# The stores of the output, issued by ScalarE at one place of the unit instead of by SyncE between the loads

## The chip, the cores and the metric

The kernel runs on one core of a Trainium2 chip. The metric is the device time of the whole kernel in microseconds. A verdict of faster or slower needs more than 2%.

## The reference

Attention over 8 batches, 12 heads, 448 positions and 64 columns a head, with one added to the softmax's denominator, and behind it one two-layer network with the activation h * tanh(softplus(h)) (Mish) on 3584 rows.

```python
scores = scale * np.matmul(q, k.transpose(0, 1, 3, 2))
m = np.max(scores, axis=-1, keepdims=True)
e = np.exp(scores - m)
attn = e / (np.sum(e, axis=-1, keepdims=True) + np.exp(-m) + 1e-09)
x = np.matmul(attn, v)           # heads side by side: [3584, 768]
h = x @ w_in                     # [768, 2048]
g = h * np.tanh(softplus(h))
out = g @ w_out                  # [2048, 768], float32
```

## The kernel before

The work is cut into units. A unit is three pairs of heads, half of a batch, so that there are 16 units of attention, u = 0 to 15 in the code. A batch's network can start when both of its units are done, so the first product with Mish runs two units behind the attention, and the second product later still. From u = 2 on a unit's stretch holds attention for itself, the end of the attention of the unit before, and the network for earlier batches. Units 16 to 19 hold the network alone.

All engines issue in the order in which the code is written. From u = 6 (`JOINED_FROM`, the seventh unit) that order is one list of steps, `JOINED`, and the loop at L738 walks it. Its steps: `s` writes scores to PSUM banks on TensorE, `m` takes row maxima on VectorE (L335), `e` the exponentials on ScalarE (L347; A and B are the two heads, the number is the step within the unit, of 12), `fill` runs two of sixteen matmuls of the second product (L543), `copy` moves finished parts of it from PSUM to an output buffer `o_sb` on VectorE (L522), `av` and `avc` are the weights times V and their copy to `xT` (L423, L432). `load` issues three loads of a pair of heads, q, k and v, on SyncE (L158), and for the second and third pair has GpSimd cast an earlier one (L201 to L207, L188). `turn` has SyncE issue a transposing DMA of one pair's q and k (L237).

Behind the list come the exponential of the maxima (L360), then the stretch from L841: eight products of the first layer (L442), each with its Mish on ScalarE (L469, L481), and between them the denominators (L363) and the normalising on VectorE and GpSimd (L386, L384), three transposing DMAs of the normalised weights on SyncE (`eT`, L390) and the transposes of the next q and k on TensorE (L224). The PSUM banks are assigned by hand: the fourth of the products goes into the bank that step 9's first head used.

A block of 128 output rows is done when 24 parts of its width have been copied. `evac` (L517) then calls `store_rows` (L495), which issues two DMAs for the block (a block spans two segments of the output), of 48 to 336 KB. They go out on SyncE's queue, at the `copy` step: behind `load` 1 and ahead of `load` 2 for the parts of `copy` 1, behind `load` 2 for those of `copy` 2. In the units u = 6, 10 and 14 one block is finished, in the other seven of u = 6 to 15 two: 17 blocks, 34 DMAs. The very last block, in pieces, has one of each two DMAs on ScalarE's queue already (L502).

`ld_pool` has four buffers for each of q, k and v, `o_pool` four.

Of the kernel before, what the change touches and what calls it, by code (L numbers as in the profile page):

```python
# [19 lines left out]
def kernel(  # L20
# [9 lines left out]
    nc = tc.nc  # L30

    B, H, S, D = q.shape
    d_model, d_ff = moe_w_in.shape
# [102 lines left out]
    def flush_late():  # L136
        while late:
            late.popleft()()
        late.extend(later)
        later.clear()  # L140

    def mo_take():

        while not mo_free:
            flush_late()
        return mo_free.popleft()
# [87 lines left out]
    def turn_by_dma(p):  # L234

        qk = qk_all[:, p % UNIT_PAIRS]
        nc.sync.dma_start_transpose(  # L237
            out=qk.rearrange("c s (t q) -> c (s t) q", q=SP_),
            in_=qk_bf[:, p % N_CAST].rearrange("q s t h d -> q (s t h d)"),
        )  # L240
        qkT[p] = qk[:, 0, :], qk[:, 1, :]
# [87 lines left out]
    def score_maxima(st, s, at, heads=(0, 1)):  # L329
        sc, cols = st["sc", s]  # L330
        maxima = [(st["negm"][:, c : c + 1], sc[bk][:, 0:S]) for bk, c in enumerate(cols) if bk in heads]
        if len(cols) == 2 and sc_pairs[at] is not None:
            maxima = [(st["negm"][:, s : s + 5 : 4], sc_pairs[at][:, :, 0:S])]
        for negm, scored in maxima:
            nc.vector.tensor_reduce(out=negm, in_=scored, axis=AX.X, op=ALU.max, negate=True)  # L335

    def exps(idx, heads=(0, 1)):
        p, s = divmod(idx, STEPS)
        if p >= N_PAIRS:
            return  # L340
        st = att[p]
        sc, cols = st["sc", s]
        rg["used"] -= 1
        for bk, c in enumerate(cols):
            if bk not in heads:
                continue
            nc.scalar.activation(  # L347
                out=st["en"][:, :, c, 0:SP_],
                in_=sc[bk][:, 0:S].rearrange("q (j c) -> q j c", j=NT),
                func=AF.Exp, bias=st["negm"][:, c : c + 1], scale=1.0,  # L350
                accum_out=st["sums"][:, c : c + 1],
            )
        if s == STEPS - 1 and p < HP:
            nc.scalar.activation(out=st["expm"], in_=st["negm"], func=AF.Exp)
        elif s == STEPS - 1 and p % UNIT_PAIRS == UNIT_PAIRS - 1 and p // UNIT_PAIRS < JOINED_FROM:
            expm_of(p)
# [56 lines left out]
    def av_pair(p, act=False, bank=None):  # L413
        b, hp = p // HP, p % HP
        eT = att[p]["eT"]
        v_bf = casted[p][2]
        if b not in xT:
            xT[b] = xT_pool.tile([128, DM_T, S], BF16, tag="xT", name="xT")
        av = mo_take() if bank is None else bank
        for j in range(NT):  # L420
            for h in range(2):
                e_h = eT[0:SP_, j, h * S : (h + 1) * S]
                nc.tensor.matmul(  # L423
                    av[h * 64 : (h + 1) * 64, 0:S],
                    lhsT=v_bf[:, h, j * D : (j + 1) * D],
                    rhs=e_h,
                    start=(j == 0), stop=(j == NT - 1),
                )
        copy = nc.scalar.copy if act else nc.vector.tensor_copy

        def evac():
            copy(out=xT[b][:, hp, :], in_=av[:, 0:S])  # L432
            if bank is None:
                mo_free.append(av)

        del att[p], casted[p], qkT[p]
        return evac
# [54 lines left out]
            out=mids[g][:, :, 64 * half : 64 * half + 64], in_=gT[b][:, :, at : at + 64]  # L492
        )

    def store_rows(g, i, o_sb, cols):  # L495

        parts, r = [], i * 128
        while r < (i + 1) * 128:
            n = min((i + 1) * 128, (r // SP_ + 1) * SP_) - r
            parts.append((r, n))  # L500
            r += n
        queues = [nc.sync, nc.scalar if (g, i) == (B // 2 - 1, 6) else nc.sync]  # L502
        for queue, (r, n) in zip(queues, sorted(parts, key=lambda part: -part[1])):
            seg = r // SP_
            b, t, c0 = 2 * g + seg // NT, seg % NT, r % SP_
            rows = out[b * S : (b + 1) * S, :].rearrange("(c t) m -> t c m", t=NT)
            queue.dma_start(
                out=rows[t, c0 : c0 + n, cols], in_=o_sb[r - i * 128 : r - i * 128 + n, cols]
            )
# [3 lines left out]
    def mm2_group(pieces, bank=None):  # L513

        st = {"at": 0, "o": bank, "evacs": []}

        def evac(g, i, q0, nq, at, last):  # L517
            cols, n_cols = slice(q0 * NQ, (q0 + nq) * NQ), nq * NQ
            if (g, i) not in o_sbs:
                o_sbs[g, i] = [o_pool.tile([128, d_model], FP32, tag="o_sb", name="o_sb"), 0]  # L520
            o_sb, have = o_sbs[g, i]
            nc.vector.tensor_copy(out=o_sb[:, cols], in_=st["o"][:, at : at + n_cols])  # L522
            if last and bank is None:
                mo_free.append(st["o"])
            o_sbs[g, i][1] = have + nq
            if (g, i) == (B // 2 - 1, 6):
                store_rows(g, i, o_sb, cols)
            elif have + nq == 24:
                store_rows(g, i, o_sb, slice(0, d_model))

        def chunk(k, f0, f1):
            g, i, q0, nq = pieces[k]
            if st["o"] is None:
                flush_late()
                st["o"] = mo_take()
            if i < 3:
                src, c0 = gT[2 * g], i * 128
            elif i == 3:
                src, c0 = mids[g], 0
            else:  # L540
                src, c0 = gT[2 * g + 1], i * 128 - S
            for ff in range(f0, f1):
                nc.tensor.matmul(  # L543
                    st["o"][:, st["at"] : st["at"] + nq * NQ],
                    lhsT=src[:, ff, c0 : c0 + 128],
                    rhs=w_out_sb[:, ff, q0 * NQ : (q0 + nq) * NQ],
                    start=(ff == 0), stop=(ff == FF_T - 1),
                )
            if f1 == FF_T:
                last = k == len(pieces) - 1  # L550
                args = (g, i, q0, nq, st["at"], last)
                st["evacs"].append(lambda: evac(*args))
                st["at"] += nq * NQ
                if last and bank is None:
                    late.extend(st["evacs"])

        step = 2
        chunks = [
            (lambda k=k, f0=f0: chunk(k, f0, f0 + step), pieces[k][3] / 6)
            for k in range(len(pieces))  # L560
            for f0 in range(0, FF_T, step)
        ]
        return chunks, st["evacs"]
# [8 lines left out]
    for g in range(B // 2):  # L572
# [61 lines left out]
        ("eB", 6), ("load", 2), ("fill", 1), ("m", 11), ("fill", 1), ("eB", 5), ("fill", 1),  # L634
# [4 lines left out]
    )  # L639
    PART_BANK = (7, 6, 2)  # L640
    AV_BANK = (7, 3, 6)
# [79 lines left out]
    for u in range(UNITS_PER_B, N_UNITS + 2 * UNITS_PER_B):  # L721
# [16 lines left out]
        for what, arg in JOINED if joined else ():  # L738
            at, idx = p0 + arg, p0 * STEPS + arg
            heads = {"A": (0,), "B": (1,)}.get(what[-1], (0, 1))  # L740
            if what == "s":
                held[arg] = score_products(idx)
            elif what[0] == "m":
                score_maxima(*held[arg], heads)
            elif what[0] == "e":
                exps(idx, heads)
            elif what == "fill":
                for _ in range(arg):
                    filler.popleft()[0]()
            elif what == "copy":  # L750
                for evac in copies[arg]:
                    evac()
            elif what == "av":
                held["av", arg] = av_pair(at - UNIT_PAIRS, bank=joined_banks[AV_BANK[arg]])
            elif what == "avc":
                held["av", arg]()
            elif what == "load":
                load_pair(at + LEAD - 1)
                if arg:
                    cast_pair(at + LEAD - 2)  # L760
            elif nxt + arg in TURN_BY_DMA:
                turn_by_dma(nxt + arg)
# [3 lines left out]
        for n in () if joined else range(steps):  # L766
            pi, s = divmod(n, STEPS)
# [73 lines left out]
        for f in range(FF_U):  # L841
# [4 lines left out]
            if moe:  # L846
                first = to_group and nxt == GROUP_FROM
                bank, ff = sc_banks[0][0] if f == 1 else None, w * FF_U + f
                if joined:
                    bank = joined_banks[JOINED_MISH_BANK[f]]  # L850
                elif to_group:
                    at = (FIRST_MISH_BANK if first else MISH_BANK)[f]
                    if at is not None:
                        bank = (sc_banks[0][1], None, mo_tiles[1], sc_banks[0][0])[at]
# [71 lines left out]
```

## Time and profile before

| | |
|---|---|
| runs | 464.16, 464.88, 459.46 us (median 464.16) |
| the profiled execution | 462.32 us; its span 460.5 us, mean granted clock 0.989 |
| TensorE busy | 427.1 us, 93% |
| VectorE, ScalarE busy | 340.7 and 342.3 us, 74% each |
| GpSimd busy | 185.7 us, 40% |
| DMA packets | 92.66 MB, mean 201 GB/s |
| units u = 6 to 15, start of the second product's first group | 145.92, 170.33, 198.50, 222.90, 247.65, 273.28, 297.68, 322.43, 346.90, 372.41 us |

Lines such as L347 are lines of the kernel. In the rows of a timeline the first number is the start and the second the duration in us; what stands in brackets is the idle time of the engine just before and what ended it. SPq and ACTq are the sequencers that issue DMAs; a DMA's row there is its issue alone, not the movement of its data. The span runs from the first to the last instruction; the execution's own time is 1.8 us longer.

### The profile page before, as it was taken

Reading aid. Unit: us, or ns where it says so; the run is one execution under the profiler, and the core shown is the slowest. Engines: PE = TensorE matmul, PEld = TensorE weight load, DVE = VectorE, ACT = ScalarE, POOL = GpSimd, SP = SyncE. Lnnn points to the kernel's source line nnn. Section 1 sums busy time; section 2 is a strip of 40 time slices with the busy share of each in tenths; the row PEclk is TensorE's granted clock in tenths of the full one; section 3 lists DMA queues with packets and bytes.
Section 4 is the critical chain, followed back from the end, with each engine's and each line's share of the span. In section 5 each row is a group of like instructions: output and inputs, shape, how many; then the busy total and the mean of one; then the engine's idle time right before and its main releaser. Section 6 shows DMA issues by size and latency. Waiting matters only on the chain.

```text
span 460.5 us, 8732 instructions
## 1 busy us (share of the span) xinstructions
PE 427.1 (93%) x2968; PEld 234.4 (51%) x2968; DVE 340.7 (74%) x756; ACT 342.3 (74%) x908; POOL 185.7 (40%) x352
## 2 busy tenths in 40 slices
PE   4586798899999999899999999999999999999996
PEld 2243445444445555455555545564555455555565
DVE  4899968878797888668788888888888888421021
ACT  5998988988797788688888887897979878211300
POOL 3666839253517161534436271715454360000000
PEclk9997999999999999999999999999999999999999
DMA  8999999997999989998999999999999995950213
GB/s 210 220 202 221 282 188 248 200 212 174 223 263 217 246 171 227 266 207 234 185 270 211 219 227 206 247 219 254 229 265 201 244 206 135 177 133 0 70 36 103
DMA packets 211661, 92.66 MB, mean 201 GB/s; under 512 B 168352, under 2 KB 208160, under 8 KB 211616
## 3 DMA queue, kind: packets, MB, share of 16 engines
q1 hardware_dynamic: 204032, 85.76, 87.4%
q0 software_dynamic: 7488, 6.29, 9.3%
q8 instruction: 23, 0.38, 0.3%
q14 instruction: 22, 0.18, 0.1%
q10 hardware_dynamic: 96, 0.05, 0.0%
HBM read 45.61 MB, written 11.01 MB: 123 GB/s over the span
## 4 chain that ended last, share of the span: by engine, by line
PE 65%; DMA 10%; DVE 9%; ACT 6%; issue 3%; SPq 3%; POOL 2%; POOLq 0%; DVEq 0%
PE mo L543 24%; PE mo L442 17%; DMA q_f<-in_q_dram 7%; PE b L442 7%; DVE negm L335 6%; PE b L543 5%; ACT en L347 5%; PE b L304 4%; PE mo L423 2%; DMA k_f<-in_k_dram 2%; PE b L224 2%; PE b L423 2%; DMA eT<-en 1%; PE mo L312 1%; DVE xT L432 1%
## 5 line engine op out<-in xcount | busy, mean ns | idle before, releaser
L347 ACT ACTIVATE en<-b,negm 128x448 bf16<-128x448 f32 x216 | 133.9, 636 | 20.9 <-DVE negm L335 20.9
L335 DVE TENSOR_REDUCE negm<-b 128x1 f32<-128x448 f32 x216 | 120.6, 614 | 21.2 <-PE b L307 21.2
L543 PE MATMUL mo<-w_out_sb,gT 128*128 128x384 bf16 (+3 forms) x736 | 107.5, 298 | 2.4 <-DVE o_sb L522 1.8
L543 PEld LDWEIGHTS <-gT 128*128 128x128 bf16 x896 | 82.4, 98 | 51.8 <-issue 10.5
L442 PEld LDWEIGHTS <-w_in_sb 128*128 128x128 bf16 x768 | 72.6, 98 | 67.7 <-issue 7.3
L442 PE MATMUL mo<-xT,w_in_sb 128*128 128x448 bf16 x480 | 102.7, 357 | 0.8 <-DVE xT L432 0.3
L481 ACT ACTIVATE gT<-mo 128x448 bf16<-128x448 f32 x73 | 40.2, 551 | 54.1 <-PE mo L442 53.7
L384 POOL TENSOR_SCALAR en<-en,rden 128x448 bf16<-128x448 bf16 x109 | 67.3, 634 | 23.5 <-DVE rden L378 15.5
L386 DVE TENSOR_SCALAR en<-en,rden 128x448 bf16<-128x448 bf16 x227 | 71.5, 384 | 0.7
L442 PE MATMUL b<-xT,w_in_sb 128*128 128x448 bf16 x282 | 58.8, 353 | 0.2 <-DVE xT L432 0.2
L347 ACT ACTIVATE en<-sc,negm 128x448 bf16<-128x448 f32 x84 | 52.5, 642 | 4.0 <-DVE negm L335 2.6
L522 DVE COPY o_sb<-mo 128x384 f32<-128x384 f32 (+3 forms) x54 | 25.8, 492 | 40.0 <-PE mo L543 39.4
L335 DVE TENSOR_REDUCE negm<-sc 128x2 f32<-128x896 f32 (+1 forms) x48 | 45.2, 966 | 6.0 <-PE sc L307 4.0
L203 POOL TENSOR_SCALAR qk_bf<-q_f 112x512 bf16<-112x512 f32 x18 | 11.1, 615 | 90.5 <-DMA q_f<-in_q_dram 90.5
L347 ACT ACTIVATION_READ_ACCUMULATOR en<-b,negm 128x1 f32 x216 | 45.1, 209 | 0.0
L188 POOL CAST v_bf<-v_f 112x512 bf16<-112x512 f32 x48 | 29.7, 619 | 14.1 <-DMA v_f<-in_v_dram 13.3
L201 POOL CAST qk_bf<-q_f 112x512 bf16<-112x512 f32 x29 | 19.2, 662 | 37.2 <-DMA q_f<-in_q_dram 36.9
L207 POOL CAST qk_bf<-k_f 112x512 bf16<-112x512 f32 x47 | 29.1, 618 | 6.0 <-DMA k_f<-in_k_dram 5.4
L224 PEld LDWEIGHTS <-qk_bf 112*128 112x128 bf16 x304 | 19.8, 104 | 22.2 <-DVE qk_bf L201 4.4
L423 PEld LDWEIGHTS <-v_bf 112*64 112x64 bf16 x384 | 20.1, 110 | 19.5 <-issue 9.2
L543 PE MATMUL b<-w_out_sb,gT 128*128 128x384 bf16 x160 | 29.3, 326 | 0.0
L304 PE MATMUL b<-qk_all 64*128 64x448 bf16 x108 | 29.0, 355 | 0.0
(71 smaller groups left out, 523.7 us busy)
## 6 DMA issues: line engine op xcount, KB each, us to landing
q_f<-in_q_dram SPq DMA_DIRECT2D x48, 224.0 KB, 5.3
k_f<-in_k_dram SPq DMA_DIRECT2D x48, 224.0 KB, 5.4
v_f<-in_v_dram SPq DMA_DIRECT2D x48, 224.0 KB, 5.6
w_in_sb<-in_moe_w_in_dram POOLq DMA_DIRECT2D x12, 256.0 KB, 6.1
w_out_sb<-in_moe_w_out_dram POOLq DMA_DIRECT2D x8, 384.0 KB, 7.7
out_dram<-o_sb SPq DMA_DIRECT2D x7, 336.0 KB, 5.1
out_dram<-o_sb SPq DMA_DIRECT2D x8, 288.0 KB, 4.8
out_dram<-o_sb SPq DMA_DIRECT2D x8, 240.0 KB, 5.4
```

The source lines that it names most:

```text
L188: nc.gpsimd.tensor_copy(out=casted[p][2], in_=loaded.pop(p)[2])
L207: cast_k(out=k_bf, in_=k_f.rearrange(by_t, t=NT))
L224: nc.tensor.transpose(by_s[s][:, t * SP_ : (t + 1) * SP_], src[:, t].rearrange("p h d -> p (h d)"), ident[:SP_, :SP_],)
L304: nc.tensor.matmul(sc[0][:, 0:S], lhsT=qT[0:64, qa : qa + 128], rhs=kA, start=True, stop=True)
L335: nc.vector.tensor_reduce(out=negm, in_=scored, axis=AX.X, op=ALU.max, negate=True)
L347: nc.scalar.activation(out=st["en"][:, :, c, 0:SP_], in_=sc[bk][:, 0:S].rearrange("q (j c) -> q j c", j=NT), func=AF.Exp, bias=st["negm"][ ...
L384: nc.gpsimd.tensor_scalar(scalar2=1.0, op0=ALU.mult, op1=ALU.mult, **args)
L386: nc.vector.tensor_scalar(scalar2=None, op0=ALU.mult, **args)
L423: nc.tensor.matmul(av[h * 64 : (h + 1) * 64, 0:S], lhsT=v_bf[:, h, j * D : (j + 1) * D], rhs=e_h, start=(j == 0), stop=(j == NT - 1),)
L442: nc.tensor.matmul(h_ps[:, 0:S], lhsT=w_in_sb[:, dm, ff * 128 : (ff + 1) * 128], rhs=xT[b][:, dm, :], start=(dm == 0), stop=(dm == DM_T - 1),)
L481: nc.scalar.activation(out=gT[b][:, ff, :], in_=h_ps[:, 0:S], func=AF.Mish)
L543: nc.tensor.matmul(st["o"][:, st["at"] : st["at"] + nq * NQ], lhsT=src[:, ff, c0 : c0 + 128], rhs=w_out_sb[:, ff, q0 * NQ : (q0 + nq) * NQ ...
```

## The change

Blocks that are finished in units from u = 6 to 15 are no longer stored at the `copy` step. They are noted in a list, and a new step `store`, at one place late in `JOINED`, issues all of them on ScalarE's queue. In ScalarE's order the place is behind the exponentials `eA 8` and ahead of `eB 9`; three more exponentials follow. In SyncE's order nothing is left of these 34 DMAs. The stores of u = 5 and before, and of u = 16 to 19, stay where they are.

```diff
+    to_store = []
+
-    def store_rows(g, i, o_sb, cols):
+    def store_rows(g, i, o_sb, cols, queue=nc.sync):
...
-        queues = [nc.sync, nc.scalar if (g, i) == (B // 2 - 1, 6) else nc.sync]
+        queues = [queue, nc.scalar if (g, i) == (B // 2 - 1, 6) else queue]
...
             elif have + nq == 24:
-                store_rows(g, i, o_sb, slice(0, d_model))
+                if bank is None:
+                    store_rows(g, i, o_sb, slice(0, d_model))
+                else:
+                    to_store.append((g, i, o_sb, slice(0, d_model), nc.scalar))
...
-        ("mB", 8), ("s", 9), ("mB", 9), ("avc", 2), ("eB", 9), ("mA", 9), ("eB", 8), ("mB", 10),
-        ("eA", 9), ("eB", 10), ("turn", 1),
+        ("mB", 8), ("s", 9), ("mB", 9), ("avc", 2), ("store", 0), ("eB", 9), ("mA", 9),
+        ("eB", 8), ("mB", 10), ("eA", 9), ("eB", 10), ("turn", 1),
...
+            elif what == "store":
+                while to_store:
+                    store_rows(*to_store.pop(0))
```

## The prediction

> I count units as the code does, from u = 0, so the seventh is u6. The ones that change are u6 to u15. In each of them the loads come as three pairs of heads; I call their transfers q0 k0 v0, q1 k1 v1, q2 k2 v2, the stores S1, S2 (one finished block of 128 rows) or S1 to S4 (two), and "the hold" the time that ScalarE is kept from its next exponential by the stores.
>
> **What bounds the kernel now.** First the page: TensorE is busy for 93% of the span and carries most of the chain that ended last; DMA carries a tenth of it.
>
> ```profile
> span 460.5 us, 8732 instructions
> PE 427.1 (93%) x2968; PEld 234.4 (51%) x2968; DVE 340.7 (74%) x756; ACT 342.3 (74%) x908; POOL 185.7 (40%) x352
> PE 65%; DMA 10%; DVE 9%; ACT 6%; issue 3%; SPq 3%; POOL 2%; POOLq 0%; DVEq 0%
> ```
>
> Then the stretches from the first matmuls of one unit's second product (the group of 32) to the next unit's: u6, u7, u10, u11 and u14. The columns are length, then busy time of PE, PEld, DVE, ACT and POOL, then the granted clock.
>
> ```profile
> 145.92:170.33 24.41, 24.41 (x174) 13.54 (x175) 21.07 (x49) 20.91 (x57) 10.06 (x21) 1.00 1.03 203
> 170.33:198.50 28.17, 26.38 (x174) 13.86 (x175) 20.62 (x48) 21.09 (x57) 14.01 (x27) 0.94 1.09 237
> ...
> 247.65:273.28 25.63, 24.75 (x174) 13.57 (x175) 21.79 (x49) 21.21 (x57) 11.58 (x24) 1.00 1.05 220
> 273.28:297.68 24.40, 24.40 (x174) 13.54 (x175) 20.84 (x48) 20.91 (x57) 10.91 (x22) 1.00 1.10 233
> ...
> 346.90:372.41 25.51, 24.34 (x166) 13.08 (x167) 21.96 (x48) 20.58 (x56) 10.91 (x22) 1.00 1.18 222
> ```
>
> A unit that nothing disturbs takes 24.40 us, all of it TensorE. So the nine units u6 to u14 (145.92 to 372.41, 226.5 us) hold only 226.5 - 9 x 24.40 = 6.9 us that any change of order could win, over half of it in u7. But two loops run close beside TensorE. The first is SyncE's queue, here in u11 with its start in the unit before:
>
> ```profile
> 268.03 13.82 SPq L390 DMA_TRANSPOSE eT<-en  x3
> 281.91 0.57 SPq L158 DMA_DIRECT2D q_f<-in_q_dram  x1
> ...
> 283.02 0.46 SPq L158 DMA_DIRECT2D v_f<-in_v_dram  x1
> 283.52 0.46 SPq L158 DMA_DIRECT2D q_f<-in_q_dram  x1
> 284.02 0.46 SPq L158 DMA_DIRECT2D k_f<-in_k_dram  x1
> 284.52 0.46 SPq L158 DMA_DIRECT2D v_f<-in_v_dram  x1
> 285.08 2.31 SPq L507 DMA_DIRECT2D out_dram<-o_sb  x4
> 287.84 0.49 SPq L158 DMA_DIRECT2D q_f<-in_q_dram  x1
> 288.85 0.34 SPq L158 DMA_DIRECT2D k_f<-in_k_dram  x1
> 289.64 0.31 SPq L158 DMA_DIRECT2D v_f<-in_v_dram  x1
> 290.30 1.27 SPq L237 DMA_TRANSPOSE qk_all<-qk_bf  x1
> 293.23 4.35 SPq L390 DMA_TRANSPOSE eT<-en  x1
> ```
>
> The transposes of the attention weights fill the queue for 13.8 us, and the loads can't start before. The second thing to see is the gaps ahead of q2, k2 and v2 (287.39 to 287.84, 288.33 to 288.85, 289.19 to 289.64). The waits of SyncE's queue in this unit name what ended them:
>
> ```profile
> SPq L158 <- DMA q_f<-in_q_dram: 0.5, 1, 0.5
> SPq L158 <- DMA k_f<-in_k_dram: 0.4, 1, 0.4
> SPq L158 <- DMA v_f<-in_v_dram: 0.4, 1, 0.4
> ```
>
> A load needs none of those transfers. GpSimd's casts, which do need them, tell when they landed:
>
> ```profile
> 287.94 0.61 POOL L188 CAST v_bf<-v_f 112x512 bf16<-112x512 f32 x1 [0.88 <-DMA v_f<-in_v_dram]
> 288.88 0.61 POOL L201 CAST qk_bf<-q_f 112x512 bf16<-112x512 f32 x1 [0.33 <-DMA q_f<-in_q_dram]
> 289.68 0.61 POOL L207 CAST qk_bf<-k_f 112x512 bf16<-112x512 f32 x1 [0.18 <-DMA k_f<-in_k_dram]
> 290.35 0.61 POOL L188 CAST v_bf<-v_f 112x512 bf16<-112x512 f32 x1
> ```
>
> q2 left when v0 had landed, k2 when q1 had, v2 when k1 had. Count the issues: v0 q1 k1 v1 S1 S2 S3 S4 q2. **Each issue waits until the transfer eight issues before it has landed.** This rule decides the case.
>
> **The change, part by part.** It takes 17 blocks, 34 DMAs, from SyncE, where they stood ahead of q2 or behind v2, and puts them on ScalarE's queue behind eA 8 and ahead of eB 9. What an issue costs:
>
> ```profile
> L507 SPq DMA_DIRECT2D out_dram<-o_sb x57: 316/424/1673, 129.9 to 457.4; - x57
> L507 ACTq EVENT_SEMAPHORE  x3: 17/17/17, 436.2 to 456.5; - x3
> L507 ACTq DMA_DIRECT2D out_dram<-o_sb x3: 376/377/395, 453.7 to 457.4; - x3
> ```
>
> Removed: about 0.42 us of SyncE's queue per store, so q2 leaves some 2.8 us sooner in u11 (behind v1 at 285.0) and lands sooner too, since the stores' data no longer go first. That ends most of the excess of u7, u10 and u14. Added on ScalarE: 0.38 us of issue per store. ScalarE has a place for it:
>
> ```profile
> 260.52 0.20 ACT L347 ACTIVATION_READ_ACCUMULATOR en<-b,negm 128x1 f32 x1
> 262.17 0.63 ACT L347 ACTIVATE en<-b,negm 128x448 bf16<-128x448 f32 x1 [1.45 <-DVE negm L335]
> ...
> 286.15 0.20 ACT L347 ACTIVATION_READ_ACCUMULATOR en<-b,negm 128x1 f32 x1
> 287.80 0.63 ACT L347 ACTIVATE en<-b,negm 128x448 bf16<-128x448 f32 x1 [1.45 <-DVE negm L335]
> ```
>
> In u10 and u11 alike it idles 1.45 us ahead of eB 9. Two issues (0.76) hide there and four (1.5) all but hide; without that cover they would be 12.9 us for all 34.
>
> **The wait that moves with them** is the cost. The question is whether ScalarE's issues count in the same eight. The trace's own records of the last issues of the kernel name the semaphore that each DMA signals on:
>
> ```
> 451.07 SP 109   451.61 SP 101   453.67 ACT 102   453.67 SP 103   454.79 SP 104
> 455.16 SP 105   456.11 ACT 107   456.10 SP 108   457.43 ACT 109   457.43 SP 101
> ```
>
> One rotation of eight (106 is no DMA's) serves both queues, and each of the three ACT issues has a wait instruction of its own ahead of it (the x3 row). So I take it that a store on ScalarE waits for the eighth DMA before it, whoever issued that one. The order around the place is eT eT eT, nine loads, the qk transpose, the stores. Eight back from S1 is v0, from S2 q1, from S3 k1, from S4 v1. ScalarE then stands still until q1 (two stores) or v1 (four) has landed, though the blocks that it stores were copied long before. In u11 that is 290.35 + 0.38 = 290.73 against 287.80 now: a hold of 2.9 us.
>
> Behind the waiting store on ScalarE are eB 9, eB 8, eA 9, eB 10, the exponential of the maxima, the table load and the first Mish. TensorE waits for eA 9's bank: the fourth product of the next stretch goes there, and its start is 288.10 + 2 x 1.14 = 290.4 by the row below, 0.7 us after eA 9 ends now (287.80 + 1.9). All but 0.7 us of the hold is TensorE's.
>
> ```profile
> 288.10 3.57 PE L442 MATMUL b<-xT,w_in_sb 128*128 128x448 bf16 x18
> ```
>
> Worse, it closes a loop: the loads land, ScalarE goes on, the sums and the normalising follow, the transposes are issued, then the next loads. From eB 9 to the first transpose takes 268.03 - 262.17 = 5.86 us; from there to v1 in hand 290.35 - 268.03 = 22.3, to q1 20.9. With the last issue (0.38) a turn of the loop is 28.6 us for four stores and 27.1 for two. In u9 it is shorter:
>
> ```profile
> 218.34 4.89 SPq L390 DMA_TRANSPOSE eT<-en  x1
> 239.84 0.61 POOL L188 CAST v_bf<-v_f 112x512 bf16<-112x512 f32 x1
> ```
>
> 21.5 to v1, so 27.7 with the same rest. I take the middle, 28.1 and 26.5. All this exceeds 24.40, so the loop, not TensorE, sets the pace. The turns that end in u7, u8, u9, u11, u12 and u13 have four stores, those in u10 and u14 two; u15 has no loads and goes free. Six at 28.1 and two at 26.5 make 221.6 us, where 346.90 - 145.92 = 201.0 stand now (the gains on q2 are swallowed in this). That is +20.6; the first hold, in u6, adds under 1, and the last slack of 0.7 is given back.
>
> Unknown costs. (a) S1 starts while q1 to v1 are under way and may slow them: from nothing to the 384 KB of a block at the 233 GB/s of u11's row, 1.6 us a turn; I take nothing, since the other side is as open: (b) if the qk transpose is counted behind S4, the wait ends with k1, 0.7 us sooner a turn. (c) An issue may meet an issue of SyncE: none to 1.27 us, the qk transpose's row; I take none, as that one starts about when v1 lands. Of this the Trainium skill speaks (Perfetto Trace Analysis, "DMA Instruction — HWDGE (DVE, Sync)"): the descriptor generator is shared by the issuing sequencers and locked for one at a time. By it the stores would cost up to a SyncE issue each, which would put the sum towards the high end; no row of this case shows such a lock.
>
> The sum against the profiled execution's own 462.3 us: 462.3 + 20.6 = **483 us**. The median of the runs shown is 464.2, so this reads as 4% slower.
>
> **Rivals.** *No hold* (not slower): ScalarE's issues do not wait for loads, because their count is kept apart. For it: 1.45 us of cover at just that place. Against it: the common rotation. Then the 6.9 us is open, less what TensorE waits in u10 for k1, which stands ahead of the stores in any case,
>
> ```profile
> 267.04 0.37 PE L224 MATMUL b<-ident,qk_bf 112*128 112x112 bf16 x4 [0.80 <-POOL qk_bf L207]
> ```
>
> and some 0.6 elsewhere: 462.3 - 5.5 = 457 us. It holds where the wait of S4 ends less than 0.7 us after eB 9's present start. The Trainium skill gives this outcome (DMA: Bandwidth & Descriptors, "Issuing engines are not separate DMA queues"): issuing from several engines saves only the sequencer's time to initiate, usually small. The 0.42 us row agrees with "small"; the rule leaves the wait ahead of an issue out.
>
> *Short hold*: in the counted order the third pair and the qk transpose come behind the stores, so S4 waits for v0 and S2 for q0. The turn with four stores is then 287.94 - 268.03 + 0.38 + 5.86 = 26.2 us, with two TensorE's 24.40: 6 x 26.2 + 2 x 24.4 - 201.0 = +5, or 467 us. Against it: without stores in front SyncE reaches q2 before ScalarE reaches the place (285.0 against 286.35).
>
> *Hold and cold clock*: now TensorE waits once for more than 1 us, in u7, and is granted about half its clock behind that.
>
> ```profile
> 192.99 0.37 PE L224 MATMUL b<-ident,qk_bf 112*128 112x112 bf16 x4 [1.61 <-POOL qk_bf L201]
> ...
> 194.00:196.00 2.00, 2.00 (x8) 0.85 (x7) 0.00 (x0) 0.98 (x2) 1.75 (x7) 0.62 1.28 290
> ```
>
> u7's 26.38 us busy against 24.41 in u6 put that at 2.0 us a unit. With such a wait in every unit the late products can delay GpSimd's share of the normalising, and with it the third transpose and the loop. If half of it enters each turn, it is 483 + 8 x 1.0 = 491 us. For the forecast I leave it out, since a turn of 28.1 has 3.7 us to spare over 24.40.
>
> **How the numbers follow.** Forecast 0.72, no hold 0.13, short hold 0.07, cold clock 0.08. The forecast's own range, from (b) on all eight turns and u9's shorter turn (475) to half of (a) (490), is 475 to 490. To hold 8 in 10 I take 466 to 495: it takes in the short hold and the cold clock and leaves out no hold. Two per cent, about what a measurement of this kernel tells from no change, is 454.9 to 473.4 about the median. Forecast and cold clock, less a little, give slower 0.77; no hold and short hold give same 0.20; 0.03 is left for faster.
>
> **What would show it.** Right: ScalarE's idle ahead of eB 9 grows from 1.45 to 3 us and more, units of 27 to 29 us from u7 to u14 and 24 in u15, TensorE waiting at L442 on ScalarE's exponentials, SyncE's queue idle ahead of the first transpose. Wrong: eB 9 still 14.5 us behind the start of its unit, and units of 24.40. Then the rotation does not bind ScalarE, and the waits for q2 will be gone from the chain.

## The result, and the profile after

The changed kernel takes 482.74 us (median of 4 runs, 480.21 to 488.37) beside 461.81 us (4 runs, 458.14 to 464.88) for the kernel before: a ratio of 1.044, interval 1.031 to 1.056. It is slower by 20 us. The ratio leaves out the run of 488.37 us, over 1.5% above the fastest; the profile shown is that of a second set of runs of the same kernel, from an execution of 482.67 us. Two of the lines have moved with the edit: the stores' L507 is now L509, the second product's L543 is L548.

First the page: span, busy times and the chain that ended last.

```profile
span 480.5 us, 8708 instructions
PE 430.8 (90%) x2968; PEld 236.1 (49%) x2968; DVE 332.5 (69%) x756; ACT 342.3 (71%) x908; POOL 185.0 (39%) x352
PE 49%; DMA 15%; SPq 13%; ACT 9%; DVE 7%; issue 3%; ACTq 1%; POOL 1%; POOLq 0%; DVEq 0%
```

The span is 20.0 us longer and hardly any of that is work: ScalarE's 342.3 us are the same to the digit, TensorE has 3.7 us more. In the chain TensorE has gone from 65% to 49%, and the transfers with SyncE's queue from 13% to 28%. This is what a path looks like that no longer runs through the busiest engine. TensorE's waits say where it joins that path:

```profile
PE b L442 <- ACT en L347: 20.3, 9, 4.2
PE sc L304 <- ACT en L347: 9.9, 13, 1.5
```

The second row stood there before with 10.0 us; the first is new, with nine waits, one in each of u6 to u14. In these nine units TensorE now waits for 20.5 us, all but 0.2 of it in the new row, where it waited for 4.1 (for GpSimd, L224). These 16.4 us and 3.1 us more of busy time (225.40 against 222.29) are the 19.5 us that the nine units have grown by. Next the timeline of ScalarE in u11, in which one row holds the case:

```profile
294.82 0.20 ACT L347 ACTIVATION_READ_ACCUMULATOR en<-b,negm 128x1 f32 x1
297.72 3.19 ACTq L509 DMA_DIRECT2D out_dram<-o_sb  x4
300.96 0.63 ACT L347 ACTIVATE en<-b,negm 128x448 bf16<-128x448 f32 x1 [5.95 <-DMA v_f<-in_v_dram]
```

eB 9 comes 5.95 us after the accumulator's read ends, 1.45 before. The four issues stand in 3.19 us, though four of the same row's median (0.36) would be 1.4: there is time between them. GpSimd's casts of the same unit say what that time is:

```profile
297.82 0.61 POOL L188 CAST v_bf<-v_f 112x512 bf16<-112x512 f32 x1 [1.03 <-DMA v_f<-in_v_dram]
298.66 0.61 POOL L201 CAST qk_bf<-q_f 112x512 bf16<-112x512 f32 x1 [0.22 <-DMA q_f<-in_q_dram]
299.56 0.61 POOL L207 CAST qk_bf<-k_f 112x512 bf16<-112x512 f32 x1 [0.29 <-DMA k_f<-in_k_dram]
300.53 0.61 POOL L188 CAST v_bf<-v_f 112x512 bf16<-112x512 f32 x1 [0.35 <-DMA v_f<-in_v_dram]
```

These are v0, q1, k1 and v1, each 0.05 to 0.12 us after it landed. By the trace's records of the semaphores they landed at 297.70, 298.61, 299.51 and 300.41 us, and the single issues are S1 297.72, S2 298.63, S3 299.53 and S4 300.43. So ScalarE issues one store for each load that lands. It is like this throughout: all 30 stores of u6 to u14 leave 0.02 us (one 0.09) after the landing of the DMA that last used their semaphore. SyncE's queue closes the loop:

```profile
270.87 1.36 SPq L237 DMA_TRANSPOSE qk_all<-qk_bf  x1
278.34 4.17 SPq L390 DMA_TRANSPOSE eT<-en  x1
...
294.89 0.46 SPq L158 DMA_DIRECT2D v_f<-in_v_dram  x1
295.39 0.46 SPq L158 DMA_DIRECT2D q_f<-in_q_dram  x1
...
306.10 4.83 SPq L390 DMA_TRANSPOSE eT<-en  x1
```

It is idle for 6.1 us ahead of the first transpose (272.23 to 278.34), and q2 now leaves right behind v1, at 295.39. From one first transpose to the next are 27.8 us. Last the stretches u6, u7, u10, u11 and u15, with the columns as before:

```profile
146.43:171.13 24.70, 24.55 (x176) 13.51 (x174) 20.49 (x49) 20.86 (x57) 10.21 (x21) 1.00 1.06 205
171.13:201.41 30.28, 26.22 (x176) 14.28 (x174) 19.78 (x48) 21.15 (x57) 13.66 (x27) 0.94 1.05 207
257.16:281.87 24.71, 24.55 (x175) 13.53 (x174) 20.59 (x49) 20.89 (x57) 8.92 (x19) 1.00 1.01 206
281.87:311.63 29.76, 25.98 (x175) 14.15 (x174) 19.79 (x48) 21.14 (x57) 13.55 (x27) 0.94 1.08 204
392.41:416.04 23.63, 23.00 (x153) 12.64 (x152) 20.56 (x51) 20.06 (x54) 3.11 (x7) 1.00 0.76 158
```

### The profile page after: what moved, and what is told of

It reads as the page before. It is cut to its first block, busy times and chain, and to the rows that moved or that the text cites. A ratio compares the mean times of both kernels' runs of the same rounds, so it can differ in the third digit from the quotient of the medians.

```text
span 486.2 us, 8708 instructions
## 1 busy us (share of the span) xinstructions
PE 431.8 (89%) x2968; PEld 236.9 (49%) x2968; DVE 333.4 (69%) x756; ACT 341.8 (70%) x908; POOL 185.5 (38%) x352
## 4 chain that ended last, share of the span: by engine, by line
PE 48%; DMA 20%; SPq 14%; ACT 10%; DVE 3%; issue 2%; POOL 1%; ACTq 1%; POOLq 0%; DVEq 0%
PE mo L548 17%; PE mo L442 15%; SPq L390 9%; DMA v_f<-in_v_dram 8%; ACT en L347 8%; PE b L442 7%; DMA eT<-en 5%; DMA k_f<-in_k_dram 5%; SPq L158 5%; PE b L304 2%; PE b L224 2%; DMA q_f<-in_q_dram 2%; DVE negm L335 2%; PE b L423 1%; ACTq L509 1%
## 5 line engine op out<-in xcount | busy, mean ns | idle before, releaser
L347 ACT ACTIVATE en<-b,negm 128x448 bf16<-128x448 f32 x216 | 133.9, 638 | 50.4 <-DMA v_f<-in_v_dram 24.7
L442 PEld LDWEIGHTS <-w_in_sb 128*128 128x128 bf16 x768 | 73.8, 100 | 92.3 <-issue 34.5
L548 PE MATMUL mo<-w_out_sb,gT 128*128 128x384 bf16 (+3 forms) x736 | 107.5, 298 | 2.4 <-DVE o_sb L524 1.8
L548 PEld LDWEIGHTS <-gT 128*128 128x128 bf16 x896 | 82.4, 98 | 51.8 <-issue 10.5
L442 PE MATMUL b<-xT,w_in_sb 128*128 128x448 bf16 x282 | 63.7, 368 | 20.7 <-ACT en L347 20.7
L386 DVE TENSOR_SCALAR en<-en,rden 128x448 bf16<-128x448 bf16 x227 | 64.6, 353 | 0.7
L524 DVE COPY o_sb<-mo 128x384 f32<-128x384 f32 (+3 forms) x54 | 25.8, 492 | 40.1 <-PE mo L548 39.5
L363 DVE SCALAR_TENSOR_TENSOR den<-sums,expm 128x21 f32<-128x21 f32 (+1 forms) x20 | 4.6, 230 | 41.6 <-ACT expm L360 41.6
L207 POOL CAST qk_bf<-k_f 112x512 bf16<-112x512 f32 x47 | 28.8, 613 | 7.2 <-DMA k_f<-in_k_dram 6.7
L201 POOL CAST qk_bf<-q_f 112x512 bf16<-112x512 f32 x29 | 17.9, 618 | 32.9 <-DMA q_f<-in_q_dram 32.1
L548 PE MATMUL b<-w_out_sb,gT 128*128 128x384 bf16 x160 | 29.3, 326 | 0.0
L224 PEld LDWEIGHTS <-qk_bf 112*128 112x128 bf16 x304 | 20.8, 108 | 17.2 <-DVE qk_bf L201 4.4
```

Of the source, the lines that this page charges most:

```text
L207: cast_k(out=k_bf, in_=k_f.rearrange(by_t, t=NT))
L224: nc.tensor.transpose(by_s[s][:, t * SP_ : (t + 1) * SP_], src[:, t].rearrange("p h d -> p (h d)"), ident[:SP_, :SP_],)
L347: nc.scalar.activation(out=st["en"][:, :, c, 0:SP_], in_=sc[bk][:, 0:S].rearrange("q (j c) -> q j c", j=NT), func=AF.Exp, bias=st["negm"][ ...
L386: nc.vector.tensor_scalar(scalar2=None, op0=ALU.mult, **args)
L442: nc.tensor.matmul(h_ps[:, 0:S], lhsT=w_in_sb[:, dm, ff * 128 : (ff + 1) * 128], rhs=xT[b][:, dm, :], start=(dm == 0), stop=(dm == DM_T - 1),)
L548: nc.tensor.matmul(st["o"][:, st["at"] : st["at"] + nq * NQ], lhsT=src[:, ff, c0 : c0 + 128], rhs=w_out_sb[:, ff, q0 * NQ : (q0 + nq) * NQ ...
```

## The experiments

The theory: a store on ScalarE waits until the DMA eight issues before it, on either queue, has landed; at this place that is a load still on its way; and since the sums, the normalising, the transposes and the next loads come behind ScalarE, this closes a loop slower than TensorE. The main rivals: that the stores' data now come late or crowd the loads, and that issuing on ScalarE is dear in itself.

The table gives each kernel's time, its ratio to the kernel before on the same chip with the interval, and the nine units u6 to u14, from the start of u6 to that of u15, in its profiled execution.

| kernel | us | ratio | nine units, us |
|---|---|---|---|
| before | 463 to 464 | 1 | 226.5 |
| changed, again | 483.1 | 1.044 [1.037, 1.051] | 246.0 |
| late_on_sp | 463.3 | 1.001 [0.996, 1.005] | 223.9 |
| read_v1 | 482.6 | 1.043 [1.037, 1.049] | 246.4 |
| read_v0 | 466.6 | 1.007 [1.002, 1.011] | 228.8 |
| read_v2 | 515.5 | 1.112 [1.103, 1.121] | 274.2 |
| split | 482.3 | 1.040 [1.030, 1.049] | 245.8 |
| act_after_expm | 466.9 | 1.007 [1.003, 1.010] | 226.7 |
| act_before_expm | 472.4 | 1.019 [1.012, 1.026] | 232.6 |
| act_prev | 544.6 | 1.177 [1.168, 1.185] | 306.1 |
| act_in_mish | 495.4 | 1.073 [1.066, 1.079] | 252.0 |
| no_stores | 461.7 | 0.997 [0.992, 1.001] | 223.4 |

The last column is of one execution each, but the sharper one. The code ahead of u6 does the same work in all of them, yet u6 starts anywhere from 145.0 to 151.3 us, and that scatter is in every span. Two profiled executions of the changed kernel, of 488.37 and 482.67 us, start u6 at 150.9 and 146.4 us and have 247.2 and 246.0 us in the nine units.

**The place without the wait, and the wait without the stores.** The changed kernel was run again, and beside it two kernels that each take half of the change. late_on_sp keeps the late step and issues on SyncE:

```diff
-                    to_store.append((g, i, o_sb, slice(0, d_model), nc.scalar))
+                    to_store.append((g, i, o_sb, slice(0, d_model), nc.sync))
```

read_v1 leaves every DMA where it was before and has ScalarE copy one column of v1 (of q1 in u6, u10 and u14) at the step; `kept` holds the loaded tiles:

```diff
+            elif what == "read":
+                if (nxt + 1, "q") in kept:
+                    nm = "q" if u in (6, 10, 14) else "v"
+                    nc.scalar.copy(out=junk[0:SP_, :], in_=kept[nxt + 1, nm][:, 0, 0:1])
```

> The changed kernel, unaltered, beside the kernel before on the same chip. Theory (each store on ScalarE waits for the DMA eight issues before it, so eB 9 waits for v1 or q1): about 4.4% over before, eB 9 starting 16 to 20 us behind the start of its unit (14.5 before), units u7 to u14 of 25.5 to 30 us. This run is also the base that the other three are compared with.

> The stores at the same late step as in the change, but issued by SyncE: only the queue is different. Theory (the wait counts because it holds ScalarE's exponentials): the wait for v1 now stands in SyncE's queue behind the third pair and the qk transpose, where 1.6 to 4.5 us of waiting for the normalising cover it; eB 9 back at 14.5 us, units of 24.4 to 24.8, time 457 to 463 us. Rival A (the cost lies in the stores' data coming late, next to the loads and the transposes): still 475 to 485 us. Rival B (nothing on SyncE covers it: the first transpose is late by four issues, 1.7 us a unit): 468 to 475 us.

> The kernel before, all stores on SyncE between the loads as before, and one more instruction on ScalarE at the place of the changed kernel's stores: a copy of one column of the landed v1 (q1 in u6, u10 and u14) into a scratch tile. It makes ScalarE wait for the same landing without issuing any DMA. Theory (it is the wait alone): about as slow as the changed kernel, 476 to 486 us, eB 9 at 16 to 20 us. Rival (it is ScalarE's issuing: a shared descriptor generator, or stores and loads mixing on two queues): 460 to 465 us.

The late place costs nothing: in the windows view of late_on_sp the nine units are even 2.6 us shorter than before.

```profile
144.96:368.86 223.90, 220.67 (x1551) 121.58 (x1550) 191.56 (x428) 188.51 (x504) 99.74 (x193) 1.00 1.09 228
```

The wait alone costs as much as the whole change. ScalarE's timeline in read_v1, in u11, shows the changed kernel's picture without a store in it:

```profile
300.95 0.19 ACT L756 COPY junk<-v_f 112x1 f32<-112x1 f32 x1 [5.98 <-DMA v_f<-in_v_dram]
301.05 0.63 ACT L350 ACTIVATE en<-b,negm 128x448 bf16<-128x448 f32 x1
```

A hold of 5.98 us beside 5.95, and 246.4 us for nine units beside 246.0. So neither late or crowding data nor the price of the issues is needed to explain the loss: waiting for v1 at this place is enough.

**More and less of the wait.** The same copy, of v0 or of v2 in every unit, makes the wait shorter or longer:

```diff
-                if (nxt + 1, "q") in kept:
+                if (nxt + 2, "v") in kept:
-                    nm = "q" if u in (6, 10, 14) else "v"
-                    nc.scalar.copy(out=junk[0:SP_, :], in_=kept[nxt + 1, nm][:, 0, 0:1])
+                    nc.scalar.copy(out=junk[0:SP_, :], in_=kept[nxt + 2, "v"][:, 0, 0:1])
```

> As the kernel before with ScalarE's one-column copy at the stores' place, but of v0 in all units instead of v1 or q1; no DMA is moved. Theory of the loop: a turn is 5.9 us from eB 9 to the first transpose, 19.8 from there to v0 in hand (287.8 - 268.0 in u11 of before) and 0.2 for the copy, 25.9 us; eight turns of 25.9 against 201 us before make +6 us, about 469 us. Rival (each hold is paid once and no loop closes): the hold of v0 is about 0.5 us behind eB 9's time in u11, within the slack of 0.7 us: no loss, 461 to 465 us.

> Edit: the kernel before, with a one-column copy of v2 by ScalarE ahead of eB 9 in u6 to u14; no DMA is moved. The wait of this case made longer by one pair. Theory (the loop of landing, exponentials, transposes, loads): v2 lands about 26.2 us behind the first transpose (294.2 against 268.03 in u11), so a turn is 26.2 + 0.2 + 5.9 = 32.3 us, and eight turns are 258 us where 201 stand: +57, 515 to 525 us. Rival (not a loop but a hold paid once a unit beyond some slack): 3.9 us more per unit than v1's hold of 2.9, less 0.7 of slack: 6.1 x 9 = +55, nearly the same time, but then each unit's loads keep their place behind the start of the unit; by the theory the transposes, the loads and eB 9 move together.

read_v0 came out between the two expectations, about 3 us above the kernel before. In u11 its wait is this row of ScalarE's timeline:

```profile
290.49 0.19 ACT L755 COPY junk<-v_f 112x1 f32<-112x1 f32 x1 [2.79 <-DMA v_f<-in_v_dram]
```

2.79 us less the 1.45 of idle that was there anyway leaves 1.3 in this unit. But the eight turns from eB 9 of u6 to that of u14 are 25.6 us in the mean (163.14 to 367.60), against 25.1 before (201.0 / 8). In seven of them eB 9 starts 0.2 us behind v0's landing, so the loop sets the pace, but it is hardly slower than the rest of the unit: from the first transpose to v0 are 19.3 us in the mean of these seven, where 19.8 were expected. By its time alone this run doesn't decide between the two expectations. read_v2 landed at the low end of its expectation. Its timelines of ScalarE and of SyncE's queue in u11:

```profile
322.40 0.19 ACT L755 COPY junk<-v_f 112x1 f32<-112x1 f32 x1 [8.59 <-DMA v_f<-in_v_dram]
322.50 0.63 ACT L350 ACTIVATE en<-b,negm 128x448 bf16<-128x448 f32 x1
```

```profile
296.56 4.21 SPq L393 DMA_TRANSPOSE eT<-en  x1
327.62 4.88 SPq L393 DMA_TRANSPOSE eT<-en  x1
```

Read it as the loop: first transpose 296.56, v2 in hand 322.40 (25.8 us), next first transpose 327.62 (5.2 us). That is a turn of 31.1 us, where 32.3 were expected: the way from eB 9 to the transpose is 5.1 and not 5.9 when everything else of the unit has been done by then. The mean of the eight turns is shorter still, 30.5 us (169.99 to 414.16); that the time came out within the expectation all the same owes something to u6, which starts 5 us later in this execution than in that of the kernel before. By its time alone this run doesn't separate the loop from a hold paid once a unit, as the expectation says; and since TensorE now waits for ScalarE, the start of the unit moves with the loop, so the place of the loads in the unit doesn't separate them either. What speaks for the loop is that each of its links waits for the one before: in all nine units eB 9 starts 0.1 us behind the start of the copy, which waits for v2, the next first transpose leaves 5.13 to 5.15 us behind eB 9, and the loads leave right behind the three transposes.

**Half of the stores.** In split the first block of a unit goes to ScalarE and the second to SyncE, so ScalarE issues 20 of the 34:

```diff
+                for queue in (nc.scalar, nc.sync):
+                    if to_store:
+                        store_rows(*to_store.pop(0), queue)
```

> The change, but where a unit has two blocks the second goes out on SyncE, at the same step: 20 stores on ScalarE in u6 to u15 instead of 34. SyncE reaches its two before ScalarE reaches its own, so in the built program the SyncE stores take the places eight behind v0 and q1, and ScalarE's two those behind k1 and v1. Theory (what holds ScalarE is the landing eight issues back, not the number of its issues): still the wait for v1, so no gain over the change, 477 to 486 us. Rival (the loss grows with the issues or the bytes on ScalarE's queue): 20 of 34, so 12 of 20 us, 472 to 475 us.

The loss is the same, 482.3 us. In the built order of this kernel ScalarE's two stores are eight behind k1 and v1, and the row of u11 shows it (k1 landed at 300.67, v1 at 301.59):

```profile
300.69 1.25 ACTq L509 DMA_DIRECT2D out_dram<-o_sb  x2
301.98 0.63 ACT L347 ACTIVATE en<-b,negm 128x448 bf16<-128x448 f32 x1 [5.56 <-DMA v_f<-in_v_dram]
```

Not how many are issued counts, but which transfer the last one has to wait for.

**Other places on ScalarE.** Four kernels have the same stores on ScalarE at other points. act_prev issues them a unit later, between the first half's `fill` steps and `copy` 1, ahead of eB 6; act_before_expm behind eB 10, ahead of the exponential of the maxima; act_after_expm behind that exponential, ahead of the table load; act_in_mish behind the seventh Mish. In all four the step `store` at its old place is gone; act_prev issues u15's blocks on SyncE at the end of u15's list.

```diff
 act_prev
-        ... ("eA", 4), ("fill", 1), ("copy", 1), ...
+        ... ("eA", 4), ("fill", 1), ("store", 0), ("copy", 1), ...
 act_before_expm, and act_after_expm with the same two lines behind L360
+            while to_store:
+                store_rows(*to_store.pop(0))
 act_in_mish
+                if f == 6 and joined:
+                    while to_store:
+                        store_rows(*to_store.pop(0))
```

> The stores on ScalarE as in the change, but issued behind the seventh Mish of the stretch that follows, some 9 us later: eight back from there are k1, v1 and later ones, which landed before. Same queue, same number of issues, no landing to wait for. Theory: no hold, 457 to 463 us, eB 9 at 14.5 us. Rival A (ScalarE's issues as such cost 34 x 0.38 = 13 us): 470 to 476 us. Rival B (an issue on ScalarE must wait while SyncE's transposes are being issued, up to 4.3 us each, since they fill the queue at that time): the issues take up to 4 us and the last Mishes are late, 470 us or more.

> The stores on ScalarE, but each unit's blocks one unit later, ahead of eB 6 some 10 us into the unit: there SyncE has just ended its transposes, and eight issues back lie k1 to v2 of the unit before, long landed. u15's blocks go out on SyncE at the end of its list. Theory: no hold and no meeting with the transposes; up to 1.5 us of issues in a busy part of ScalarE, which the 1.45 us of idle time ahead of eB 9 takes up: 458 to 467 us. Rival (ScalarE's queue as such costs, in issues or by mixing stores with loads): 472 us or more.

> Edit: the same stores on ScalarE behind eB 10 and ahead of the exponential of the maxima, one step earlier than in the run above. Theory: the wait for v1 is back in a loop, now through the exponential of the maxima alone. If the sums need that exponential, a turn is 22.3 (first transpose to v1) + 0.4 + 3.4 (from there to the next transpose, since eB 9 to eB 10 are done) = 26.1 us for four stores, so six turns lose 1.7 each: +5 to +10 us, 465 to 473 us. Rival: the wait costs the same wherever ScalarE stands in it, 480 us and more.

> Edit: the same stores on ScalarE, at the end of the stretch instead: behind eB 10 and the exponential of the maxima, ahead of the table load and the first Mish. Theory (a store holds ScalarE until its eight back, v0 to v1, have landed, and the loss comes from the exponentials that stand behind it): v1 lands about when this place is reached, and no exponential of the loop is behind it, so there is no turn of 28 us; units of 24.4 to 25.5 us, 460 to 466 us, eB 9 about 14.5 us behind the start of its unit. Rival (issuing on ScalarE is dear wherever it stands, by its meeting SyncE's transposes as in the Mish): 475 us and more, with issues on ScalarE of over 1 us.

Two of the four expectations failed outright, and a third was missed by 1 us. act_prev was meant to wait for nothing and came out slowest of all, because the count was taken wrongly: in its built order eight back are k0, q1, k1 and v1 of the same unit, and the place is earlier in the stretch. ScalarE's timeline, in u8:

```profile
219.89 4.42 ACTq L509 DMA_DIRECT2D out_dram<-o_sb  x4
224.37 0.63 ACT L347 ACTIVATE en<-b,negm 128x448 bf16<-128x448 f32 x1 [8.78 <-DMA v_f<-in_v_dram]
```

v1 landed at 223.82, S4 left at 223.84. So it is the theory's own loop with more of the stretch behind the wait: about 16 us from v1 to the next first transpose (223.82 to 240.09) in place of 5.7, and nine units of 306 us.

act_before_expm and act_after_expm are one step apart, and both came out where the loop puts them, the second 1 us above its expectation. Ahead of the exponential of the maxima the wait for v1 is still in the loop, with little behind it:

```profile
290.69 2.22 ACTq L509 DMA_DIRECT2D out_dram<-o_sb  x3
292.96 0.22 ACT L360 ACTIVATE expm<-negm 128x21 f32<-128x21 f32 x1 [2.56 <-DMA v_f<-in_v_dram]
```

```profile
270.13 4.24 SPq L390 DMA_TRANSPOSE eT<-en  x1
296.33 5.00 SPq L390 DMA_TRANSPOSE eT<-en  x1
```

A turn of 26.2 us where 26.1 were expected, and nine units 6.1 us longer than before. Behind that exponential ScalarE still waits, here for a transfer of the third pair,

```profile
293.45 1.33 ACTq L509 DMA_DIRECT2D out_dram<-o_sb  x2
294.82 1.28 ACT L481 ACT_TABLE_LOAD   x1 [2.16 <-DMA q_f<-in_q_dram]
```

but what waits with it is the table load of the Mish, not the sums, and the nine units of its windows view are those of the kernel before:

```profile
149.11:375.76 226.65, 221.24 (x1552) 121.76 (x1550) 191.04 (x428) 187.29 (x504) 100.47 (x196) 1.00 1.09 225
```

Its median is still 0.7% above the kernel before. The profiled execution has its 3 us ahead of u6, where the code is the same, so where the runs lose them isn't settled.

act_in_mish came out as rival B of its expectation had it, with long issues. Its stores wait for no load (ScalarE's timeline, in u6):

```profile
168.57 5.60 ACTq L509 DMA_DIRECT2D out_dram<-o_sb  x2
174.22 0.54 ACT L481 ACTIVATE gT<-mo 128x448 bf16<-128x448 f32 x1 [5.11 <-PE mo L548]
```

but two issues last 5.60 us. SyncE's queue issues its transposes just then:

```profile
165.83 15.11 SPq L390 DMA_TRANSPOSE eT<-en  x3
```

The groups of the two lines, min, median and max in ns, from u6 on in act_in_mish:

```profile
L509 ACTq DMA_DIRECT2D out_dram<-o_sb x34: 322/1174/4422, 168.6 to 425.3; - x34
L390 SPq DMA_TRANSPOSE eT<-en x31: 4114/4426/9091, 143.7 to 424.1; - x31
```

beside the stores of the changed kernel, and the transposes of the kernel before and of late_on_sp, from u6 on:

```profile
L509 ACTq DMA_DIRECT2D out_dram<-o_sb x37: 321/359/1126, 160.6 to 477.4; - x37
```

```profile
L390 SPq DMA_TRANSPOSE eT<-en x30: 4145/4344/5291, 144.3 to 392.1; - x30
```

```profile
L390 SPq DMA_TRANSPOSE eT<-en x30: 4122/4287/6599, 143.8 to 388.8; - x30
```

Where stores on ScalarE meet transposes on SyncE, both kinds of issue last longer. Twelve of act_in_mish's transposes last over 5.5 us, all with a store issued or its data still moving beside them; in the kernel before none does. That the issues themselves hold one another isn't shown. In late_on_sp, whose stores leave on SyncE just ahead of the transposes, three transposes last 5.5 to 6.6 us too, so stores whose data are still moving can be enough. How much of the 32 us is ScalarE's hold and how much the later transposes wasn't separated.

**What there was to win.** no_stores leaves the stores of the blocks finished in u6 to u15 away altogether, so these rows aren't written:

```diff
-                store_rows(g, i, o_sb, slice(0, d_model))
+                if bank is None:
+                    store_rows(g, i, o_sb, slice(0, d_model))
```

> The kernel before without the 34 stores of u6 to u15: these rows of the output are not written. It gives what any place for them could win at most. By the units' excess over 24.40 us in the trace of before (6.9 us, of which 0.8 and some more wait for k1) about 5.5 us: 455 to 459 us. If the stores are hidden already: 461 to 465 us.

461.7 us, not to be told from the kernel before (interval 0.8% below to 0.1% above); its nine units are 3.1 us shorter than before. By these two executions that is about what the best of places for these stores could win.

## Why the prediction was right, and where its sizes were off

483 us were predicted, 482.7 measured, for the predicted reason: read_v1 gives the same time from the wait alone. That the two agree to 0.3 us is luck, since the parts of the sum were off by up to 0.7 us a turn each and made up for one another.

- *The rule of eight, and that both queues share the count*: right. It was read from the semaphores of the kernel's last DMAs and the gaps in SyncE's queue; S1 to S4 leaving as v0, q1, k1 and v1 land, and the same in all 30 stores of u6 to u14, is the direct sight of it.
- *The loop*: right. From eB 9 of u6 to that of u14 are 221.4 us, where 221.6 were predicted; the turns with four stores take 28.1 us in the mean (27.4 to 28.8), those with two 26.4, predicted 28.1 and 26.5 (the prediction doesn't work out the 26.5; by the middle that it took for four stores, with q1 20.1 us behind the first transpose in u9, it would be 26.7, 0.4 us more in the sum). Of these two, only the one in u10 waits for q1 as counted (26.0); in u14 a second transpose of q and k is counted ahead of the stores, and S2 leaves as k1 lands, at 382.91 (26.8). The parts, with the prediction's value in brackets: from first transpose to v1 21.6 to 22.6 (22.3), from eB 9 to the transpose 5.1 to 5.7 (5.86), the last issue and the step to eB 9 0.4 to 1.0 (0.38).
- *The first hold under 1 us, u15 free*: right. eB 9 of u6 starts 0.9 us later in its unit, and u15 takes 23.63, where it took 23.57 before (372.41 to 395.98).
- *Units of 27 to 29 us*: not so. They alternate, 24.7, 30.3, 25.7, 30.1, 24.7 and so on. A unit is marked at the second product, which is not in the loop; the turns from eB 9 to eB 9 are the steady measure. ScalarE's idle ahead of eB 9 is 3.3 to 6.4 us in seven of the nine units, as foreseen, but only 2.3 in u6 and u10.
- *Cold clock*: the mechanism is there and stays out of the turn, as argued. In u7, u9 and u11, in which TensorE waits 3.8 to 4.2 us for ScalarE, the granted clock is 0.94 and TensorE is busy for 25.9 to 26.2 us; in u6 and u10, where it waits 0.15, 1.00 and 24.55. So it is three units, not all nine, and TensorE's busy time in the nine is 3.1 us above that of the kernel before.
- *Unknown costs*: (a) left nothing on the turn beyond the scatter of its parts, and (b) didn't come up: in all six units with four stores S4 leaves as v1 lands. (c), longer issues where the two queues meet, is there, as act_in_mish shows, but small at this place: the longest of ScalarE's issues is 1.13 us, the median 0.36. The Trainium skill (Perfetto Trace Analysis, "DMA Instruction — HWDGE (DVE, Sync)") has two issuing sequencers share one descriptor generator; the issues of up to 4.42 us in act_in_mish are in keeping with that, but no run here shows that the generator is what holds them.
- *What was to be won* was the mis-sized term. 5.5 of the 6.9 us of excess were taken as winnable by a better order, which gave 457 us for no hold. late_on_sp is that case with SyncE as issuer, q2 right behind v1: u7 lost its excess (24.40 us), as the step said, but u11 to u13, 24.4 to 24.8 before, rose to between 25.05 and 25.52, the time is 463.3, and no_stores bounds the gain at about 3 us. It didn't enter the forecast, since the loop covers it.

## What to carry to other kernels

An issue that moves to another queue takes its wait along: count in the built order which transfer stands as many issues back as there are completion semaphores, look up when that one lands, and look at what stands behind the issue on its new engine. Ahead of the last instruction that starts the next round, such a wait closes a loop and is paid in every turn; one step behind that instruction it costs little, as act_before_expm and act_after_expm show. And compare stretches from the first changed unit on, since a span also carries scatter from ahead of it.

## What the runs showed of the hardware

The wait ahead of an issue goes by the completion semaphore, also where another engine issued the transfer that used it last: all 30 stores that the changed kernel issues on ScalarE in u6 to u14 leave 0.02 us (one 0.09) after the DMA that last used their semaphore, which SyncE had issued, has landed.

Issues on ScalarE and SyncE can last longer where they meet. In act_in_mish a store's issue on ScalarE took up to 4.42 us with a median of 1.17 from u6 on, where the changed kernel has a median of 0.36, and a transpose's issue on SyncE up to 9.09 us, where the kernel before has at most 5.29 from u6 on. Whether it is the issues or the stores' data that hold the transposes stays open; late_on_sp, with the stores on SyncE, has transposes of up to 6.60 us. So a second queue was not free here even for an engine with idle time, where transposing DMAs are issued beside it.
